# Chunk inverses of a gated linear attention stored as 32x32 blocks, and applied by 32-row, 32-column matmuls

## The chip, the cores and the metric

The kernel runs on one core of a Trainium2 chip. The core has a matrix engine (TensorE, PE in the profile, with its weight loads as PEld), a vector engine (VectorE, DVE), a scalar engine (ScalarE, ACT), GpSimd (POOL), and DMA queues, some of them issued by SyncE (SP). The engines run on their own and meet at semaphores. The metric is the time of one execution in microseconds (us) on the device; lower is better.

## The reference

A recurrent attention over 768 tokens for 4 x 8 heads of 40 dimensions, followed by a mixture of 8 experts over the 3,072 tokens that it gives. Cut to what matters:

```python
for t in range(S):                      # S = 768
    y[:, :, t] = einsum('bhd,bhde->bhe', rt, state)
    Sa = einsum('bhde,bhe->bhd', state, at)
    state_decay = state * wt[:, :, None, :] - einsum('bhd,bhe->bhde', Sa, bt)
    state = state_decay + einsum('bhd,bhe->bhde', vt, kt)
...
x = attn_out.transpose(0, 2, 1, 3).reshape(B * S, H * D)
# tokens with x @ w_skip > 0 go to their best expert:
h = np.maximum(xc[mask] @ w1[e], 0.0)
out[do_compute] = xc + gate_w[mask, None] * (h @ w2[e])
```

## The kernel before, in words

The 768 tokens are worked in 24 chunks of 32. Within a chunk the recurrence becomes matrix products, but for one thing: token t removes what the earlier tokens of its chunk have already removed. That is a triangular system of 32x32 per head and chunk, and its inverse is computed once and then applied to a block of right-hand sides. A chunk has 32 such systems (4 batches x 8 heads). The heads go as two halves, x = 0 and x = 1, of four heads each, and in each half four 32x32 inverses of one head, one for each batch, are applied together.

**The inverse.** `tinv` (L210) is a generator that makes the inverses of two pairs of chunks (one phase, four chunks) by elimination on VectorE: thirty steps of a product (L228) and a subtraction (L230), spread over the chunks by calls of `T()`, each of which takes one step. Batches lie on the partitions in blocks of 32. At the end ScalarE copies a piece (L232), and L237 transposes the result into the tiles `TBa`. `TBa[q]` holds the inverses of one pair of chunks, [128 partitions, 16, 128]: entry [p, h, m] is a 128x128 matrix for each h, with the four 32x32 inverses of the batches on its diagonal and zeros elsewhere. L237 takes one batch at a time: it reads 32 partitions and writes them into their 32 columns of both tiles. What is left of the generator when a phase ends is run at once (`run_all(tg)`), so the transposes stand between the end of one phase's last chunk and the start of the next phase. The zeros off the diagonal were put there at the start: by ScalarE for `TBa[0]` (L391), by GpSimd for `TBa[1]` (L425) and for `TBa[2]` (L540, in chunk 2). The inverses of the first phase come from `tinv0` (L239), whose parts `full` (L271) and `s2` (L275) copy pieces into `TBa` with VectorE and ScalarE in turn.

**Applying it.** For chunk c and half x, in this order: `rs` (L284) multiplies the state with r, its result copied by VectorE (L296) or ScalarE (L297); `ux` (L299) makes the right-hand sides (L306), copied by ScalarE (L308); `uq` (L310) applies the inverse (L315): four matmuls, one per head, with the whole 128x128 block-diagonal matrix as weights and 72 columns moving; ScalarE copies the result out in four pieces (L317) and GpSimd masks a part of it (L319); `sst` (L320) makes the new state (L327, L332), copied by L336, L337 and L340; `yy` (L342) makes the output (L350, L354). A matmul in fp32 shows as two matmul and two weight-load instructions in the profile.

**The order.** TensorE, ScalarE and VectorE run what is written, in the order in which it is written, chunk by chunk in the loop from L469 on; no scheduler moves anything. Between the steps of the chain lie the preparation of later chunks (L163 and its transposes L174, `kbt` L185 and L188, `wtt` L197, `m2` L207, scans L114 and L126, GpSimd's L143, L151 and L170) and the routing of finished tokens to the experts (`route`, called by `RP`: L632, L640, L675, L676 on TensorE, L648 to L685 on VectorE, the scattered write L688 on GpSimd). `warm` and `zb` (L358) are matmuls with no use of their own. The experts (L786, L797) follow after the last chunk.

Names in the profile: `TB` the inverses, `M` a work area, `UXs` the copied right-hand sides, `pc`, `ps`, `py`, `pq`, `px` PSUM banks, `R1t` and `L2t` operands of the chain, `SS` the state.

## Time and profile before

| what | value |
|---|---|
| timed runs, median (lowest to highest of 3) | 689.55 us (689.51 to 695.32) |
| profiled execution: its time, its span | 686.84 us, 685.0 us |
| granted TensorE clock, mean | 0.842 |
| busy: PE, PEld | 553.0 us (81%), 473.5 us (69%) |
| busy: DVE, ACT, POOL | 516.1 us (75%), 422.7 us (62%), 324.2 us (47%) |
| instructions | 31,223, of them 13,620 matmuls |
| attention, about | 0 to 540 us of the span |
| experts, about | 540 to 685 us |

The profile was taken of one execution, and the durations in the text are of that execution. Its time is the span and 1.8 us around it. In the tables by line a row reads: line, engine, operation, written tile <- read tiles, shapes, count, then busy time in us, mean ns of one instruction, idle time of the engine ahead of them and what ended it. In the stretches in order of time the two numbers ahead are the start and the length in us, and what stands in brackets is the engine's idle time ahead of the row and what ended it. The chain of work that ended last is followed back from the end of the program: at each step to what released it, or to the instruction ahead of it on its engine. The granted clock is 1 at the full speed of TensorE and 0.5 at the half; it changes between these two during the attention.

### The profile page before, as it was taken

Reading aid. Unit: us, or ns where it says so; the run is one execution under the profiler, and the core shown is the slowest. Engines: PE = TensorE matmul, PEld = TensorE weight load, DVE = VectorE, ACT = ScalarE, POOL = GpSimd, SP = SyncE. Lnnn points to the kernel's source line nnn. Section 1 sums busy time; section 2 is a strip of 40 time slices with the busy share of each in tenths; the row PEclk is TensorE's granted clock in tenths of the full one; section 3 lists DMA queues with packets and bytes.
Section 4 is the critical chain, followed back from the end, with each engine's and each line's share of the span. In section 5 each row is a group of like instructions: output and inputs, shape, how many; then the busy total and the mean of one; then the engine's idle time right before and its main releaser. Section 6 shows DMA issues by size and latency. Waiting matters only on the chain.

```text
span 685.0 us, 31223 instructions
## 1 busy us (share of the span) xinstructions
PE 553.0 (81%) x13620; PEld 473.5 (69%) x13620; DVE 516.1 (75%) x1201; ACT 422.7 (62%) x1154; POOL 324.2 (47%) x248
## 2 busy tenths in 40 slices
PE   5678586778776789866898678997978799999995
PEld 2445475667665668655787567776767689999995
DVE  7999678876997779977699774785339366889881
ACT  6545564576864758747687475877686454444540
POOL 5483942736546365463554533131322236666661
PEclk9788878578996777969779687798897999999998
DMA  7672755352443514435244242435256347677210
GB/s 185 185 239 98 194 138 180 109 161 58 125 132 102 163 50 121 141 102 166 60 129 131 73 126 71 104 110 185 73 158 170 108 127 221 215 214 226 87 49 23
DMA packets 67437, 90.91 MB, mean 133 GB/s; under 512 B 32564, under 2 KB 54657, under 8 KB 65806
## 3 DMA queue, kind: packets, MB, share of 16 engines
q1 hardware_dynamic: 62350, 74.05, 37.2%
q0 software_dynamic: 4944, 14.80, 6.8%
q8 instruction: 109, 1.79, 1.1%
q14 instruction: 34, 0.28, 0.1%
HBM read 74.03 MB, written 17.08 MB: 133 GB/s over the span
## 4 chain that ended last, share of the span: by engine, by line
PE 37%; DVE 29%; ACT 11%; issue 10%; DMA 4%; POOL 3%; POOLq 0%; DVEq 0%; ACTq 0%
DVE M L228 5%; PE pc L786 4%; PE pc L315 4%; PE ps L797 4%; DVE M L126 4%; DVE TB L237 4%; ACT R1t L317 3%; PE ps L327 3%; PE pc L306 3%; PE px L786 2%; PE pc L292 2%; DVE M L230 2%; PE py L797 2%; PE ps L332 2%; ACT L2t L188 2%
## 5 line engine op out<-in xcount | busy, mean ns | idle before, releaser
L319 POOL TENSOR_TENSOR R1t<-R1t,mc 64x512 f32<-64x512 f32 x46 | 62.2, 1353 | 152.2 <-ACT R1t L317 123.7
L317 ACT COPY R1t<-pc 32x288 f32<-32x288 f32 x192 | 74.8, 389 | 30.6 <-PE pc L315 27.5
L315 PE MATMUL pc<-UXs,TB 128*128 128x72 f32 x384 | 66.4, 328 | 0.1
L143 POOL TENSOR_TENSOR WR<-WR,M 128x1024 f32<-128x1024 f32 (+1 forms) x19 | 52.0, 2748 | 23.0 <-DVE M L114 16.9
L734 POOL TENSOR_TENSOR WL<-WR,WH 128x1280 fp32r<-128x1280 f32 (+1 forms) x21 | 57.6, 2779 | 8.7 <-ACT WH L733 8.6
L327 PE MATMUL ps<-R1t,L2t 128*40 128x40 f32 x1472 | 52.4, 228 | 10.9 <-ACT R1t L317 5.1
L315 PEld LDWEIGHTS pc<-UXs,TB 128*128 128x128 f32 x384 | 58.8, 234 | 3.4 <-issue 1.0
L188 ACT COPY L2t<-pq 64x160 f32<-64x160 f32 x184 | 52.6, 286 | 7.0 <-PE pq L185 4.7
L327 PEld LDWEIGHTS ps<-R1t,L2t 128*40 128x40 f32 x1472 | 42.7, 139 | 20.3 <-ACT R1t L317 11.7
L209 ACT COPY R1t<-pq 32x128 f32<-32x128 f32 x184 | 47.0, 256 | 6.5 <-issue 3.0
L228 DVE TENSOR_TENSOR M<-M 128x22 f32<-128x22 f32 (+10 forms) x110 | 49.7, 452 | 0.0
L237 DVE STREAM_TRANSPOSE TB<-M 32x1024 f32<-32x1024 f32 x20 | 38.4, 1919 | 13.7 <-ACT M L232 13.5
L292 PE MATMUL pc<-rvt,SS 128*40 128x32 f32 x1472 | 44.9, 218 | 3.7 <-issue 3.6
L340 ACT COPY SS<-ps 40x320 f32<-40x320 f32 x92 | 38.6, 419 | 14.5 <-PE ps L332 13.0
L688 POOL DMA_INDIRECT xg<-XS,ix x24 | 25.0, 1040 | 46.5 <-DMA xg<-XS,ix 20.9
L292 PEld LDWEIGHTS pc<-rvt,SS 128*40 128x40 f32 x1472 | 38.6, 137 | 11.7 <-issue 8.7
L332 PE MATMUL ps<-L2t,R1t 128*40 128x40 f32 x1472 | 42.7, 220 | 0.4 <-issue 0.4
L308 ACT COPY UXs<-pc 128x288 f32<-128x288 f32 x48 | 19.2, 400 | 36.1 <-PE pc L306 32.1
L230 DVE TENSOR_TENSOR px<-px,M 128x168 f32<-128x168 f32 (+8 forms) x150 | 39.1, 261 | 1.4
L733 ACT CAST WH<-WR 128x1024 fp32r<-128x1024 f32 (+1 forms) x35 | 39.6, 1132 | 0.0
L332 PEld LDWEIGHTS ps<-L2t,R1t 128*40 128x40 f32 x1472 | 38.8, 136 | 0.5 <-issue 0.5
L228 DVE TENSOR_TENSOR M<-M,px 128x168 f32<-128x168 f32 (+8 forms) x150 | 37.0, 247 | 1.7
(244 smaller groups left out, 1577.5 us busy)
## 6 DMA issues: line engine op xcount, KB each, us to landing
rvt<-rv POOLq DMA_DIRECT2D x21, 512.0 KB, 4.6
WR<-kb SPq DMA_DIRECT2D x10, 1024.0 KB
WR<-w SPq DMA_DIRECT2D x16, 640.0 KB
WR<-w SPq DMA_DIRECT2D x16, 512.0 KB
M<-wt SPq DMA_DIRECT2D x9, 520.5 KB
M<-at SPq DMA_DIRECT2D x8, 512.0 KB
WR<-w SPq DMA_DIRECT2D x16, 256.0 KB
R1t<-vt SPq DMA_DIRECT2D x48, 80.0 KB
```

The source lines that it names most:

```text
L143: E.tensor_tensor(H[h]['KB'][0:NR(h),:,:,q,:],H[h]['KB'][0:NR(h),:,:,q,:],v4(Wi)[0:NR(h)],ALU.mult)
L188: A.copy(L2[x][h%NL2][64-64*x:128-64*x,c,bb*4:bb*4+4,:],pt[64*c:64*c+64,:,64*x:64*x+40])
L228: V.tensor_tensor(tv,NLt[:,j,j+1:32].unsqueeze(2).broadcast_to([128,n,k]),X[:,j,lo:hi].unsqueeze(1).broadcast_to([128,n,k]),ALU.mult)
L230: for tv,xv in q: V.tensor_tensor(xv,xv,tv,ALU.subtract)
L237: V.transpose(d.rearrange("p h (x f) m -> p m x h f",x=2)[:,q],Xi[q])
L292: TE.matmul(RS[s,v,:],SS[x][:,b//2,v,:],rr[:,b%2,2*hh+x,:],start=True,stop=True)
L315: TE.matmul(UQ[:,hh,:],Tb[:,x*8+hh*2+c%2,:],UXd[x][:,hh,:],start=True,stop=True)
L317: A.copy(R[uu,4*b:4*b+4,:],UQ[32*b:32*b+32,:,:])
L319: (V if c==NC-1 else G).tensor_tensor(R[pq,:,40:72],R[pq,:,40:72],mQ[pq].unsqueeze(1).broadcast_to([64,16,32]),ALU.mult)
L327: TE.matmul(ST[s,v,:],l2[:,cc,u,:],R[:,u,0:40],start=True,stop=True)
L332: TE.matmul(S2[s,v,:],R[:,u,0:40],l2[:,cc,u,:],start=True,stop=True)
L734: def low(s,E,o,x,h): E.tensor_tensor(s.R(o),x,h,ALU.subtract)
```

## The change

The inverses are kept as 32x32 blocks without the zeros around them: `TBa[q]` is [128, 16, 32], a quarter of the size, and entry [p, h, m] holds batch p // 32's inverse alone. `uq` issues sixteen matmuls for four: for each head and each batch b one with the 32 rows and 32 columns at 32b, on the diagonal of the array. L237's four transposes of 32 partitions become one of 128, with one step of the generator for four, and with writes that lie 32 elements apart instead of 128. `full` copies all 128 partitions with one VectorE copy for four copies (two of them on ScalarE in its first call). With no zeros to keep, the three clearings of `TBa` go. Scratch that had lain in `TBa[2]` before it was first used lies in a tile of its own, `SCR`.

```diff
-    TB=cp.tile([128,NTB*2048],F32,name="TB")
-    TBa=[TB[:,2048*q:2048*q+2048].rearrange("p (h m) -> p h m",h=16) for q in range(NTB)]
+    TB=cp.tile([128,NTB*512],F32,name="TB"); SCR=cp.tile([128,2048],F32,name="SCR")
+    TBa=[TB[:,512*q:512*q+512].rearrange("p (h m) -> p h m",h=16) for q in range(NTB)]
...
         s0=(2*ph)%NTB; s1=(2*ph+1)%NTB
-        for b in range(4):
-            q=slice(32*b,32*b+32)
-            t0=TBa[s0]; d=bass.AP(t0.tensor,t0[q].offset,(tuple(t0[q].ap[0]),(TBa[s1].offset-t0.offset,2),(128,16),(1,128)))
-            V.transpose(d.rearrange("p h (x f) m -> p m x h f",x=2)[:,q],Xi[q])
-            yield
+        t0=TBa[s0]; d=bass.AP(t0.tensor,t0.offset,(tuple(t0.ap[0]),(TBa[s1].offset-t0.offset,2),(32,16),(1,32)))
+        V.transpose(d.rearrange("p h (x f) m -> p m x h f",x=2),Xi)
+        yield
...
-        DB=TBa[2][:,12:16].rearrange("p h m -> p (h m)").rearrange("p (a b) -> p a b",a=16)
+        DB=SCR[:,1536:2048].rearrange("p (a b) -> p a b",a=16)
...
-        def full(w,E):
-            for b in range(4):
-                q=slice(32*b,32*b+32)
-                (V.tensor_copy,A.copy)[E[b]](TBa[w][q,:,q].rearrange("p (x f) m -> p x f m",x=2),NLt[q].rearrange("p m (x h f) -> p h x f m",x=2,h=2)[:,w])
+        def full(w):
+            V.tensor_copy(TBa[w].rearrange("p (x f) m -> p x f m",x=2),NLt.rearrange("p m (x h f) -> p h x f m",x=2,h=2)[:,w])
...
         for hh in range(4):
-            TE.matmul(UQ[:,hh,:],Tb[:,x*8+hh*2+c%2,:],UXd[x][:,hh,:],start=True,stop=True)
+            for b in range(4):
+                q=slice(32*b,32*b+32)
+                TE.matmul(UQ[q,hh,:],Tb[q,x*8+hh*2+c%2,:],UXd[x][q,hh,:],start=True,stop=True)
...
-            zero(fT(0))
...
-            G.memset(fT(1),0.0); G.memset(z[:,512:640],0.0); G.memset(L1t[:,2048:3072],0.0)
+            G.memset(z[:,512:640],0.0); G.memset(L1t[:,2048:3072],0.0)
...
-            full(0,(0,1,0,1))
+            full(0)
...
-            if c==1: full(1,(0,0,0,0)); m1(3,0,0); m1(3,0,1)
+            if c==1: full(1); m1(3,0,0); m1(3,0,1)
...
-            if c==2: s2(1,1,(0,0,1,1)); G.memset(TBa[2],0.0)
+            if c==2: s2(1,1,(0,0,1,1))
```

On VectorE, where chunk 7 ends and chunk 8 begins (230 us in the profile), the order before was as follows; the transposes write `TB`, the rows on `R1t` are evacuations of the chain, and those on `pos`, `base`, `sl` and `ix` are the routing:

```order
L354 TENSOR_TENSOR XS<-py_103,WT 128x320
L237 STREAM_TRANSPOSE TB<-M 32x32x2x2x8
L336 TENSOR_TENSOR R1t<-ps_102,D_977 40x8x40 x2
L237 STREAM_TRANSPOSE TB<-M 32x32x2x2x8 x3
L680 TENSOR_TENSOR pos<-pq_105,base 128x8
L681 TENSOR_TENSOR base<-pq_105,base 128x8
L680 TENSOR_TENSOR pos<-pq_105,base 128x8
```

And at the same place in the changed kernel, whose lines have other numbers (L235 is the transpose, L334 what was L336, L676 and L677 what were L680 and L681):

```order
L352 TENSOR_TENSOR XS<-py_103,WT 128x320
L235 STREAM_TRANSPOSE TB<-M 128x32x2x2x8
L334 TENSOR_TENSOR R1t<-ps_102,D_985 40x8x40 x2
L676 TENSOR_TENSOR pos<-pq_105,base 128x8
L677 TENSOR_TENSOR base<-pq_105,base 128x8
L676 TENSOR_TENSOR pos<-pq_105,base 128x8
```

The one transpose stands where the first of the four stood, and the three behind the evacuation are gone; all else keeps its order.

On TensorE, at the start of chunk 8, the order before, in which L315 applies the inverse for the second half of chunk 7 (each row is one matmul of the program, times the count):

```order
L676 MATMUL pq_105<-oh,mc 32x16 x4
L292 MATMUL pc_100<-rvt,SS_115 40x32 x16
L163 MATMUL pq_104<-WR,L1t 32x64 x16
L315 MATMUL pc_99<-UXs,TB 128x72 x4
L197 MATMUL pq_105<-mc,WE 128x104 x4
L350 MATMUL py_103<-L2t,R1t 32x40 x16
L632 MATMUL pq_104<-mc,XS 128x128 x2
```

And in the changed kernel (L313 is what was L315):

```order
L672 MATMUL pq_105<-oh,mc 32x16 x4
L288 MATMUL pc_100<-rvt,SS_116 40x32 x16
L163 MATMUL pq_104<-WR,L1t 32x64 x16
L313 MATMUL pc_99<-UXs,TB 32x72 x16
L197 MATMUL pq_105<-mc,WE 128x104 x4
L348 MATMUL py_103<-L2t,R1t 32x40 x16
L628 MATMUL pq_104<-mc,XS 128x128 x2
```

Sixteen matmuls of 32x72 stand where four of 128x72 stood, between the same neighbours.

## The prediction

> **What bounds the kernel now.** I read the chain of work that ended last first, then one of its stretches in order of time, and then the same stretch on all engines. The chain, by engine and by line:

> ```profile
> PE 37%; DVE 29%; ACT 11%; issue 10%; DMA 4%; POOL 3%; POOLq 0%; DVEq 0%; ACTq 0%
> by line: issue 9.9%; DVE M L228 5.0%; PE pc L786 4.2%; PE pc L315 4.2%; PE ps L797 4.1%; DVE M L126 3.9%; DVE TB L237 3.7%; ACT R1t L317 3.4%; PE ps L327 3.3%; PE pc L306 2.8%; PE px L786 2.5%; PE pc L292 2.4%; DVE M L230 2.2%; PE py L797 2
> ```

> No engine is the bound by itself; the chain hops between TensorE, VectorE and ScalarE. Both lines that the change rewrites stand on it: L315, the matmuls that apply the inverse, with 4.2% of 685.0 us = 28.8 us, and L237, the transposes that write the inverse out, with 3.7% = 25.3 us. The groups of the same trace (count | busy us, mean ns), with a third line to measure L237 by:

> ```profile
> L315 PE MATMUL pc<-UXs,TB 128*128 128x72 f32 x384 | 66.4, 328 | 0.1
> L237 DVE STREAM_TRANSPOSE TB<-M 32x1024 f32<-32x1024 f32 x20 | 38.4, 1919 | 13.7 <-ACT M L232 13.5
> L213 DVE STREAM_TRANSPOSE M<-M 128x1024 f32<-128x1024 f32 x5 | 6.1, 1211 | 0.0
> ```

> So 25.3 of L237's 38.4 us are on the chain. The twenty transposes come as four at each of five places, where one pair of chunks ends and the next begins (144, 230, 316, 400 and 472 us). The second of them, all engines, start and duration in us:

> ```profile
> 229.98 0.37 ACT L232 COPY M<-px 128x256 f32<-128x256 f32 x1
> 230.38 1.91 DVE L237 STREAM_TRANSPOSE TB<-M 32x1024 f32<-32x1024 f32 x1 [3.03 <-ACT M L232]
> 232.16 0.95 DVE L336 TENSOR_TENSOR R1t<-ps,D 40x320 f32<-40x320 f32 x2
> 233.13 5.79 DVE L237 STREAM_TRANSPOSE TB<-M 32x1024 f32<-32x1024 f32 x3
> 233.22 0.29 PE L676 MATMUL pq<-oh,mc 128*32 128x16 f32 x8
> 233.44 1.28 PE L292 MATMUL pc<-rvt,SS 128*40 128x32 f32 x32
> 234.65 1.08 PE L163 MATMUL pq<-WR,L1t 128*32 128x64 f32 x32
> 235.66 1.99 PE L315 MATMUL pc<-UXs,TB 128*128 128x72 f32 x8
> 238.94 0.17 DVE L680 TENSOR_TENSOR pos<-pq,base 128x8 f32<-128x8 f32 x1
> 239.50 0.96 PE L197 MATMUL pq<-mc,WE 104*128 104x104 f32 x4 [1.85 <-DVE base L681]
> 240.39 0.76 PE L350 MATMUL py<-L2t,R1t 128*32 128x40 f32 x32
> 240.98 0.85 DVE L296 TENSOR_TENSOR R1t<-pc,D 40x256 f32<-40x256 f32 x2
> 242.23 0.90 PE L632 MATMUL pq<-mc,XS 128*128 128x128 f32 x3 [1.08 <-DVE M L174]
> 243.07 1.19 PE L306 MATMUL pc<-R1t,WR 128*32 128x72 f32 x32
> ```

> VectorE is busy with transposes until 238.92; the routing step L680 and L681, whose input (L676) was there at 233.51, queues behind them. TensorE has run ahead, finishes L315 at 237.65, and waits 1.85 us for L681; L296, which feeds the next chunk's first matmuls L306, is late for the same reason. The place is VectorE's.

> **The change, part by part.** *The transposes.* Four instructions of 32 partitions become one of 128 with as many elements each. The trace has no transpose of 128 partitions into this layout: L237 itself (1.92 us, scattered writes) and L213 (1.21 us, contiguous) are the nearest on either side. I take 1.92 us, since the writes stay scattered, only 32 elements apart instead of 128. VectorE is then rid of 3 x 1.92 = 5.8 us at each place: 28.8 us of busy time.

> Not all of that is worth time, since TensorE is close behind. In the stretch above the one transpose ends at 230.38 + 1.92 = 232.30, L336 at 233.3, the routing steps L680 to L685 took 240.98 - 238.94 = 2.04 us and end at 233.51 + 2.04 = 235.6, L296 at 236.4. The end is now set on TensorE, which goes on from L315 at 235.66: the new L315 (1.19 us at this clock, below), L197 0.96, L350 0.76, L632 0.90, so L306 starts at 239.47 instead of 243.07: 3.6 us. For the other places, L315 and L306:

> ```profile
> 149.22 1.98 PE L315 MATMUL pc<-UXs,TB 128*128 128x72 f32 x8
> 156.62 1.19 PE L306 MATMUL pc<-R1t,L1t 128*32 128x72 f32 x32
> 321.09 1.11 PE L315 MATMUL pc<-UXs,TB 128*128 128x72 f32 x8
> 327.86 1.19 PE L306 MATMUL pc<-R1t,L1t 128*32 128x72 f32 x32
> 405.75 1.57 PE L315 MATMUL pc<-UXs,TB 128*128 128x72 f32 x8
> 412.73 1.19 PE L306 MATMUL pc<-R1t,WR 128*32 128x72 f32 x32
> 475.72 0.78 PE L197 MATMUL pq<-mc,WE 104*128 104x104 f32 x3 [2.93 <-issue]
> ```

> The same 3.81 us behind L315 give 3.6, 3.0 and 3.2 us. The fifth place is held by TensorE's own wait at 475.72, so there I count only the shorter L315, 0.8 us. Together 3.6 + 3.6 + 3.0 + 3.2 + 0.8 = 14.2 us. At the full clock the 3.81 us would shrink, at most to some 2.4, which bounds the term at 20; if ScalarE's queue holds TensorE back by a further us at each place, it is 10.

> *The matmuls.* An old step is 4 matmuls of 128x128 weights, 8 instructions; a new one is 16 of 32x32, 32 instructions. Nothing in the trace has exactly that shape, but L306 has the same count and the same 72 moving columns, with four column tiles in turn. Both, at the full and at the half clock:

> ```profile
> 223.88 1.11 PE L315 MATMUL pc<-UXs,TB 128*128 128x72 f32 x8
> 229.80 0.71 PE L306 MATMUL pc<-R1t,L1t 128*32 128x72 f32 x32
> ```

> Full: 1.11 becomes 0.71, 0.40 saved. Half (rows at 235.66 and 243.07 above): 1.99 becomes 1.19, 0.80 saved. That is 36% and 40% of a step, and so 0.38 x 28.8 = 10.9 us if all of L315's share of the chain follows; 0.8 of it is counted already. TensorE's order is fixed and the steps beside it often wait for somebody else (L306 for VectorE, L327 for ScalarE's L317), so I take two thirds of 10.1, 6.7 us, with 3.4 and 10.1 as the ends.

> Is L306 a fair price? It uses four column strips and all rows; the new matmuls use four different row strips and four column strips, and all four write into one PSUM bank. The chunk-inverse start-up has just that diagonal pattern, with 16 columns (L269); the warm-up matmuls give the time per column without tiles:

> ```profile
> 60.35 1.29 PE L269 MATMUL pq<-M 32*16 32x16 f32 x128
> 66.67 2.84 PE L358 MATMUL ps<-mc 128*128 128x512 f32 x6
> ```

> L358 takes 2.84 / 6 = 0.47 us for 512 columns, 0.92 ns a column. Sixteen columns one after another would be 14.8 ns; L269 starts one every (1.29 - 0.18) / 127 = 8.7 ns. So diagonal tiles overlap. [...]

> *Instructions.* TensorE gets 48 x 24 = 1,152 more matmul instructions on 13,620, and as many weight loads. It stops at times with nothing to wait for, as 2.93 us in the row at 475.72. One such stop more is 2.9 us, none is 0; I take 1.5 us lost.

> *Start-up.* L274's copies become one for each half. The second half stands on VectorE while GpSimd's small L132 copies are on the chain:

> ```profile
> 76.57 2.36 DVE L274 COPY TB<-M 32x512 f32<-32x512 f32 x4
> ```

> ```profile
> 77.22 0.56 POOL D L132
> 79.02 0.18 POOL D L132
> ```

> L132 takes 0.56 us beside L274 and 0.18 without it. Three of the four copies go, with one L132 beside each: 3 x (0.56 - 0.18) = 1.1 us gained, between 0 and 1.5. The cleared TB areas go too. I price them at nothing: ScalarE's 1.89 us lie before a 5.91 us idle stretch, GpSimd's at L425 before one of 12.75 us, and the one at L540 stands between its own steps at 127 us, with nobody waiting; without that cover they would be worth 1.8 us each.

> ```profile
> 19.73 0.60 ACT L165 COPY M<-pq 128x128 f32<-128x128 f32 x2 [5.91 <-issue]
> 62.21 2.90 POOL L319 TENSOR_TENSOR R1t<-R1t,mc 64x512 f32<-64x512 f32 x1 [12.75 <-issue]
> 126.82 1.83 POOL L540 MEMSET TB<- 128x2048 f32 x1
> ```

> The sum: 14.2 + 6.7 + 1.1 - 1.5 = 20.5 us off the profiled execution's 686.84, that is 666.3. That execution lies 2.7 us below the median of the timed runs, 689.55; against the median, 669.0. With all ends the gain is 10 + 3.4 + 0 - 2.9 = 10.5 to 20 + 10.1 + 1.5 = 31.6 us: 658 to 679.

> **The rivals.** *Row tiles do not overlap (slower).* If the four diagonal matmuls ran one after another, a column at 0.92 ns, a step would take 32 x 72 x 0.92 ns = 2.1 us at the full clock and twice that at the half: 1.4 and 3.0 us over my 0.71 and 1.19. The 28.8 us on the chain are about 19 steps of 1.5 us, and four more lie at the places above, so each 0.1 us a step costs 2.3 us. At a mean of 2.2 us over, 51 us are lost against 20.5 gained: 720. It decides from about 0.9 us over, where the gain is used up: an instruction every 45 ns at the full clock instead of 16. For it: no row shows 32x32 tiles with 72 columns. Against it: L269. Chance 0.05.

> *The clock.* In two stages (length, TensorE busy, ..., then the granted clock):

> ```profile
> 230.00:316.00 86.00, 68.62 (x2064) 58.53 (x2059) 71.03 (x187) 57.85 (x176) 43.31 (x36) 0.76 0.39 116
> 540.00:685.00 145.00, 133.37 (x1099) 127.45 (x1087) 100.55 (x146) 63.27 (x92) 75.30 (x39) 0.98 0.47 143
> ```

> The clock stood at 0.98 where TensorE was busy for 92% of the stage and at 0.76 where it was for 80%. Some 130 of the chain's 253 us on TensorE (37% of 685) lie before the last stage. If smaller matmuls cost clock, 0.76 to 0.68, these take 130 x (0.76 / 0.68 - 1) = 15 us more: a gain of 5, 684; chance 0.06. The reverse: TensorE no longer idles 1.85 us and more at the five places, and the half clock behind them (L306 1.19 instead of 0.71) stays away for some six groups of 0.48 us each: 14 us more gained, 655; chance 0.12. Busy time speaks for neither: per stage about 5 us go from 68.6 and about 5 from 86, which leaves 0.79 against 0.80.

> *Another chain is close behind.* ScalarE's L317 copies and GpSimd's L319 follow each step unchanged. If they eat half of the first term and all of the second, 7 + 1 - 1.5 = 6.5 us are left: 683. Chance 0.15.

> **How the numbers follow.** Forecast 0.62 (658 to 679), more clock 0.12 (655), close chain 0.15 (683), less clock 0.06 (684), no overlap 0.05 (720). The range 654 to 682 holds the first two and leaves out most of the rest. One per cent, about what a measurement of this kernel can tell from no change, is 6.9 us: faster means below 682.7. The first two cases and about half of the close chain are faster, 0.81; its other half and nearly all of less clock are the same, 0.13; slower is 0.06.

> **What would show it.** Right: five transposes of 128x1024 near 1.9 us each; L680 starting as soon as L676 and L336 are done; TensorE going from the inverse matmuls to L197 without a wait for VectorE; those steps at 0.7 and 1.2 us. Wrong: steps of 2 us and more, a granted clock under 0.70 in 230 to 316, or a ScalarE wait of several us in the place of VectorE's.

## The result and the profile after

The changed kernel takes 663.96 us (median of 4 runs, 661.24 to 667.34) against 691.1 us for the kernel before, run beside it (689.51 to 695.32): a ratio of 0.960, 95% interval 0.954 to 0.967. Run again in a later comparison it took 665.85 us against 689.88, a ratio of 0.966 (0.959 to 0.973). The gain is 24 to 27 us, 3.4 to 4%. Ratios leave disturbed runs out, which matters for one kernel below, the one with twelve short extra matmuls: two of its four runs are left out, and its ratio answers to 677 us where the median of all four is 682.43. The profiled execution took 663.83 us, with a span of 662.1 us: 23.0 us below the profiled execution of before.

More lines of the changed kernel have new numbers: L302 was L306, L292 was L296, L330 was L332, L348 was L350. The first rows of its page, with the row of the queue that brings instructions (packets, MB, share):

```profile
span 662.1 us, 33508 instructions
PE 515.5 (78%) x14772; PEld 432.2 (65%) x14772; DVE 489.7 (74%) x1182; ACT 419.5 (63%) x1151; POOL 324.2 (49%) x246
q8 instruction: 118, 1.93, 1.2%
```

The chain of work that ended last can be followed back in this trace only to 315 us, so its shares cannot be set beside those of before. TensorE's busy time fell by 37.5 us although it has 1,152 more matmul instructions, and VectorE's by 26.4 us. The instruction queue brought 9 packets more than the row below, from the page of before:

```profile
q8 instruction: 109, 1.79, 1.1%
```

1.93 MB in 118 packets is 16.4 KB each, and 1,152 matmuls over 9 packets are 128 a packet: with the weight load of each, 256 of TensorE's instructions for each packet. Two kernels below agree: with 1,152 matmul instructions more than the changed kernel the queue brings 127 packets, with 588 fewer 113. The number comes back below.

The rewritten groups of the changed kernel:

```profile
L313 PE MATMUL pc<-UXs,TB 32*32 32x72 f32 x1536 | 43.1, 255 | 6.0 <-issue 5.9
L235 DVE STREAM_TRANSPOSE TB<-M 128x1024 f32<-128x1024 f32 x5 | 9.8, 1960 | 13.9 <-ACT M L232 13.9
```

The inverse matmuls went from 66.4 to 43.1 us; the transposes from 38.4 to 9.8, and one of 128 partitions, at 1.96 us, costs what one of 32 did (1.92). Now the second phase end, where chunk 7 gives way to chunk 8, in order of time. It answers to the stretch at 230 us of before:

```profile
220.78 0.37 ACT L232 COPY M<-px 128x256 f32<-128x256 f32 x1
221.18 1.96 DVE L235 STREAM_TRANSPOSE TB<-M 128x1024 f32<-128x1024 f32 x1 [3.04 <-ACT M L232]
222.98 0.96 DVE L334 TENSOR_TENSOR R1t<-ps,D 40x320 f32<-40x320 f32 x2
...
223.98 0.23 PE L672 MATMUL pq<-oh,mc 128*32 128x16 f32 x8
...
224.35 0.17 DVE L676 TENSOR_TENSOR pos<-pq,base 128x8 f32<-128x8 f32 x1 [0.42 <-PE pq L672]
...
225.47 0.86 DVE L292 TENSOR_TENSOR R1t<-pc,D 40x256 f32<-40x256 f32 x2
...
226.43 1.18 PE L313 MATMUL pc<-UXs,TB 32*32 32x72 f32 x32
227.54 0.58 PE L197 MATMUL pq<-mc,WE 104*128 104x104 f32 x4
228.05 0.34 PE L348 MATMUL py<-L2t,R1t 128*32 128x40 f32 x14
230.40 0.40 PE L348 MATMUL py<-L2t,R1t 128*32 128x40 f32 x18 [2.00 <-issue]
230.73 0.71 PE L628 MATMUL pq<-mc,XS 128*128 128x128 f32 x3
231.37 1.19 PE L302 MATMUL pc<-R1t,WR 128*32 128x72 f32 x32
```

The routing step L676 now starts as soon as L672 has its sums, with VectorE idle ahead of it; L313 runs straight into L197, where TensorE had waited 1.85 us for L681. From the first transpose to L302 it is 231.37 - 221.18 = 10.19 us, where before it was 243.07 - 230.38 = 12.69. So 2.5 us came of the 3.6 forecast for this place; a new stop of 2.00 us, in the middle of L348 and ended by nothing the profile shows, fell into the gap.

The same two things over the whole run, in the list of TensorE's waits (who waits <- for what: us in total, times, longest). Before:

```profile
PE pc L306 <- DVE R1t L296: 17.7, 7, 4.4
PE pq L197 <- DVE base L681: 9.4, 4, 3.2
PE pq L163 <- issue: 3.9, 6, 1.4
PE py L350 <- issue: 3.7, 2, 2.6
```

After:

```profile
PE pc L302 <- DVE R1t L292: 11.0, 7, 2.9
PE pq L163 <- issue: 11.1, 10, 3.3
PE py L348 <- issue: 8.6, 7, 2.0
PE ps L330 <- issue: 6.4, 4, 3.5
```

The wait for the routing's `base` is gone from the list, and the one of L306 for L296 is 6.7 us shorter: 16.1 us together. (In the second profile of the changed kernel the latter is 14.2 us, 3.5 shorter.) Of all of TensorE's waits for VectorE, 64 us became 46 in both profiles. Stops that nothing explains grew from 25.0 to 53.4 us in total (47.1 in the second profile of the same kernel). That is where the change costs time, and the experiments below are mostly about it.

### The profile page after: what moved, and what is told of

It reads as the page before. It is cut to its first block, busy times and chain, and to the rows that moved or that the text cites. A ratio compares the mean times of both kernels' runs of the same rounds, so it can differ in the third digit from the quotient of the medians.

```text
span 662.1 us, 33508 instructions
## 1 busy us (share of the span) xinstructions
PE 515.5 (78%) x14772; PEld 432.2 (65%) x14772; DVE 489.7 (74%) x1182; ACT 419.5 (63%) x1151; POOL 324.2 (49%) x246
## 3 DMA queue, kind: packets, MB, share of 16 engines
q8 instruction: 118, 1.93, 1.2%
## 4 chain that ended last, share of the span: by engine, by line
PE 24%; DVE 11%; ACT 8%; issue 5%; DMA 2%; POOL 1%; SPq 0%; POOLq 0%; DVEq 0%; ACTq 0%
PE pc L782 5%; PE ps L793 4%; PE px L782 3%; ACT R1t L315 2%; PE py L793 2%; ACT L2t L188 2%; DVE M L228 2%; PE ps L325 2%; DVE ti L789 2%; PE pc L313 1%; PE pc L288 1%; DVE M L230 1%; PE ps L330 1%; ACT SS L338 1%; ACT R1t L209 1%
## 5 line engine op out<-in xcount | busy, mean ns | idle before, releaser
L317 POOL TENSOR_TENSOR R1t<-R1t,mc 64x512 f32<-64x512 f32 x46 | 60.5, 1315 | 104.7 <-ACT R1t L315 72.6
L315 ACT COPY R1t<-pc 32x288 f32<-32x288 f32 x192 | 74.9, 390 | 20.7 <-PE pc L313 17.6
L325 PE MATMUL ps<-R1t,L2t 128*40 128x40 f32 x1472 | 48.2, 221 | 11.0 <-issue 5.3
L143 POOL TENSOR_TENSOR WR<-WR,M 128x1024 f32<-128x1024 f32 (+1 forms) x19 | 44.2, 2332 | 25.8 <-DVE M L114 19.7
L228 DVE TENSOR_TENSOR M<-M 128x22 f32<-128x22 f32 (+10 forms) x110 | 55.0, 500 | 0.0
L325 PEld LDWEIGHTS ps<-R1t,L2t 128*40 128x40 f32 x1472 | 39.3, 132 | 18.9 <-ACT R1t L315 8.9
L330 PE MATMUL ps<-L2t,R1t 128*40 128x40 f32 x1472 | 42.9, 218 | 6.5 <-issue 6.4
L313 PE MATMUL pc<-UXs,TB 32*32 32x72 f32 x1536 | 43.1, 255 | 6.0 <-issue 5.9
L330 PEld LDWEIGHTS ps<-L2t,R1t 128*40 128x40 f32 x1472 | 38.2, 134 | 7.3 <-issue 7.2
L230 DVE TENSOR_TENSOR M<-M 128x22 f32<-128x22 f32 (+10 forms) x110 | 40.8, 371 | 0.0
L230 DVE TENSOR_TENSOR px<-px,M 128x168 f32<-128x168 f32 (+8 forms) x150 | 39.1, 260 | 1.4
L313 PEld LDWEIGHTS pc<-UXs,TB 32*32 32x32 f32 x1536 | 32.1, 122 | 11.4 <-issue 8.9
L789 DVE CAST ti<-xe 128x2 int32<-128x2 f32 x8 | 39.3, 4911 | 0.2
L174 DVE STREAM_TRANSPOSE M<-pq 128x128 f32<-128x128 f32 x40 | 12.1, 308 | 36.9 <-ACT M L165 24.3
```

The source lines that it names most:

```text
L228: V.tensor_tensor(tv,NLt[:,j,j+1:32].unsqueeze(2).broadcast_to([128,n,k]),X[:,j,lo:hi].unsqueeze(1).broadcast_to([128,n,k]),ALU.mult)
L230: for tv,xv in q: V.tensor_tensor(xv,xv,tv,ALU.subtract)
L313: TE.matmul(UQ[q,hh,:],Tb[q,x*8+hh*2+c%2,:],UXd[x][q,hh,:],start=True,stop=True)
L315: A.copy(R[uu,4*b:4*b+4,:],UQ[32*b:32*b+32,:,:])
L317: (V if c==NC-1 else G).tensor_tensor(R[pq,:,40:72],R[pq,:,40:72],mQ[pq].unsqueeze(1).broadcast_to([64,16,32]),ALU.mult)
L325: TE.matmul(ST[s,v,:],l2[:,cc,u,:],R[:,u,0:40],start=True,stop=True)
```

## Experiments

The line numbers of before hold for the first two kernels, those of the changed kernel (shifted by a few where lines were added) for the others. Each time is a median beside runs of the kernel before on the same chip: 688.42 us in the comparison with the first four, 689.88 with the next four, 690.33 with the last three.

### One part alone: the matmuls

The kernel before, with `uq` as sixteen 32x32 matmuls that read the blocks out of the wide, zero-filled tiles. Four transposes, clearings and copies stay.

```diff
         for hh in range(4):
-            TE.matmul(UQ[:,hh,:],Tb[:,x*8+hh*2+c%2,:],UXd[x][:,hh,:],start=True,stop=True)
+            for b in range(4):
+                q=slice(32*b,32*b+32)
+                TE.matmul(UQ[q,hh,:],Tb[q,x*8+hh*2+c%2,q],UXd[x][q,hh,:],start=True,stop=True)
```

> The kernel before with the sixteen 32x32 matmuls alone (weights cut out of the wide block-diagonal tiles; four transposes, start-up and clearings as before). My theory: shorter matmuls are worth little by themselves, because TensorE gets 1,152 more matmul instructions and waits for instruction blocks more often (its idle time with no releaser goes from 25 us to 45 us or more), and because VectorE still holds the phase ends: 686 to 692 us against 690. The prediction's own terms (6.7 less 1.5) would give 685. The rival, that the matmuls carry the gain: 680 or less.

681.83 us, a ratio of 0.989 (0.982 to 0.997): 6.6 us gained, with some 2 to 12 as the interval. The matmuls alone help, by about the forecast's net of 6.7 - 1.5 = 5.2, and the expectation of 686 to 692 failed; the unexplained stops came to 40.2 us, where it said 45 or more. That they are waits for blocks of instructions is its theory; what the traces show of it stands at the end. At the second phase end the four transposes and the wait behind them are as before:

```profile
225.63 5.78 DVE L237 STREAM_TRANSPOSE TB<-M 32x1024 f32<-32x1024 f32 x3
231.99 0.95 PE L197 MATMUL pq<-mc,WE 104*128 104x104 f32 x4 [2.68 <-DVE base L683]
```

### One part alone: the transposes

The kernel before with three of the four transposes of each place left out, so the inverses of batches 1 to 3 are not written behind the first phase. The 128x128 matmuls stay.

```diff
-        for b in range(4):
+        for b in range(1):
             q=slice(32*b,32*b+32)
```

> The kernel before with one of the four transposes at each phase end left out of four (one of 32 partitions runs, three are left out, so three batches keep stale inverses). Nothing else is changed. My theory: the phase ends carry most of the gain, 672 to 677 us (14 to 18 us off, as in the prediction's first term or a little over). The rival, that the matmuls carry it: 683 or more.

673.69 us, 0.978 (0.970 to 0.986): 14.7 us, beside the 14.2 of the forecast's first term. The two are not quite the same thing. The 14.2 us count on the shorter inverse matmul at each place, which this kernel does not have; with L315 as long as before, the prediction's rows give 2.8, 2.8, 3.0, 2.8 and 0 us for the five places, 11.4 together. From the first transpose of a place to the next L306, its profile takes 3.6, 3.1, 3.5, 2.8 and 3.1 us less than that of before, 16.1 together. So the fifth place, priced at nothing but the shorter L315, gives as much as the others. It begins and ends here, and in the profile of before at 472.31 and 482.77:

```profile
461.84 1.91 DVE L237 STREAM_TRANSPOSE TB<-M 32x1024 f32<-32x1024 f32 x1 [2.53 <-ACT M L232]
469.21 0.84 PE L306 MATMUL pc<-R1t,L1t 128*32 128x72 f32 x32
```

At the second place TensorE stops in the middle of L350, as it does in L348 of the changed kernel:

```profile
234.07 0.61 PE L350 MATMUL py<-L2t,R1t 128*32 128x40 f32 x19 [1.68 <-issue]
```

### The same from the other side: four transposes in the changed kernel

```diff
-        t0=TBa[s0]; d=bass.AP(t0.tensor,t0.offset,(tuple(t0.ap[0]),(TBa[s1].offset-t0.offset,2),(32,16),(1,32)))
-        V.transpose(d.rearrange("p h (x f) m -> p m x h f",x=2),Xi)
-        yield
+        for b in range(4):
+            q=slice(32*b,32*b+32)
+            t0=TBa[s0]; d=bass.AP(t0.tensor,t0[q].offset,(tuple(t0[q].ap[0]),(TBa[s1].offset-t0.offset,2),(32,16),(1,32)))
+            V.transpose(d.rearrange("p h (x f) m -> p m x h f",x=2),Xi[q])
+            yield
```

> The changed kernel with its one transpose split again into four of 32 partitions, into the narrow tiles. My theory: VectorE holds the phase ends again, some 14 to 18 us of the 27 are lost: 677 to 682 us. The rival (matmuls carry the gain): below 670.

681.51 us, 0.989 (0.982 to 0.997): 16 to 17.5 us more than the changed kernel's 665.85 and 663.96, and the wait is back where it was.

```profile
226.85 5.79 DVE L237 STREAM_TRANSPOSE TB<-M 32x1024 f32<-32x1024 f32 x3
233.22 0.96 PE L197 MATMUL pq<-mc,WE 104*128 104x104 f32 x4 [3.61 <-DVE base L679]
```

This kernel has the small matmuls and the narrow tiles and stands where the matmuls alone stood (681.83). So the larger part of the gain is the transposes', from either side.

### The start-up

The changed kernel with the old start-up: four copies for each half, two of them on ScalarE, and the three clearings, of a tile that nothing reads.

```diff
-    TB=cp.tile([128,NTB*512],F32,name="TB"); SCR=cp.tile([128,2048],F32,name="SCR")
+    TB=cp.tile([128,NTB*512],F32,name="TB"); SCR=cp.tile([128,2048],F32,name="SCR"); DUM=cp.tile([128,2048],F32,name="DUM")
...
-        def full(w):
-            V.tensor_copy(TBa[w].rearrange("p (x f) m -> p x f m",x=2),NLt.rearrange("p m (x h f) -> p h x f m",x=2,h=2)[:,w])
+        def full(w,E):
+            for b in range(4):
+                q=slice(32*b,32*b+32)
+                (V.tensor_copy,A.copy)[E[b]](TBa[w][q].rearrange("p (x f) m -> p x f m",x=2),NLt[q].rearrange("p m (x h f) -> p h x f m",x=2,h=2)[:,w])
...
+            zero(DUM)
...
-            G.memset(z[:,512:640],0.0); G.memset(L1t[:,2048:3072],0.0)
+            G.memset(DUM,0.0); G.memset(z[:,512:640],0.0); G.memset(L1t[:,2048:3072],0.0)
...
-            full(0)
+            full(0,(0,1,0,1))
...
-            if c==1: full(1); m1(3,0,0); m1(3,0,1)
+            if c==1: full(1,(0,0,0,0)); m1(3,0,0); m1(3,0,1)
...
-            if c==2: s2(1,1,(0,0,1,1))
+            if c==2: s2(1,1,(0,0,1,1)); G.memset(DUM,0.0)
```

> The changed kernel with the start-up work of before: four copies in each half of the start-up inverse, and three clearings of the old size (of a tile that nothing reads). The prediction's term: 1.1 us lost, 665. The rival, read from the trace (chunk 1's first inverse step begins 5.3 us earlier after the change): 4 to 7 us lost, 668 to 671.

664.22 us, 0.964 (0.956 to 0.971): no difference from 663.96 and 665.85. A loss of 4 to 7 us is ruled out; one of 1.1 us would be too small to tell from nothing in these runs.

### What the extra instructions cost

Two kernels with nearly the same extra array work in each of the 48 steps of `uq` and very different counts: twelve extra matmuls of one column, or one extra matmul of 112 columns. What they add goes to a part of the PSUM tile that nothing reads. Both are edits of the changed kernel, whose own time in this comparison is 665.85 us.

> The changed kernel once more, as the base of the three beside it: 661 to 667 us.

```diff
-        UQ=ps_c.tile([128,4,72],F32,tag="pc",name="psUQ")
+        UQf=ps_c.tile([128,512],F32,tag="pc",name="psUQ"); UQ=UQf[:,0:288].rearrange("p (a b) -> p a b",a=4)
...
+        for k in range(12):
+            q=slice(32*(k%4),32*(k%4)+32)
+            TE.matmul(UQf[q,288+k:289+k],Tb[q,x*8+c%2,:],UXd[x][q,0,k:k+1],start=True,stop=True)
```

> The changed kernel with twelve more 32x32 matmuls of one moving column at each inverse step, into unused PSUM columns: 24 matmul instructions and 24 weight loads, some 24 x 8.7 ns = 0.2 us of array time. If TensorE is held by the supply of instructions: 8 to 15 us slower than the changed kernel, and the idle time of TensorE with no releaser rises from 53 us to 75 or more. If only array time counts: 2 to 5 us slower, as the next kernel.

A ratio of 0.981 (0.974 to 0.989), that is 677 us (682.43 as the median of all four, from 674.6 to 687.2): 11 us more than the changed kernel. The unexplained stops came to 71.6 us in its profile, a run of 687.18 us; 75 or more were expected. And with one long matmul in their place:

```diff
+        TE.matmul(UQf[0:32,288:400],Tb[0:32,x*8+c%2,:],UXd[x][0:32].rearrange("p h n -> p (h n)")[:,0:112],start=True,stop=True)
```

> The changed kernel with one more 32x32 matmul of 112 moving columns at each inverse step: 2 matmul instructions and 2 weight loads, some 2 x 103 ns = 0.2 us of array time, as in the kernel beside it. Supply of instructions: 1 to 4 us slower than the changed kernel, clearly less than the short ones. Array time alone: the same as the short ones.

670.29 us, 0.973 (0.968 to 0.977), that is 671 us by the ratio: 4.4 us more, a little over the 1 to 4 expected. The added groups, the short ones first and the long one in the second fence (of the first row only the count and the busy time are used):

```profile
L316 PE MATMUL pc<-UXs,TB 32*32 32x1 f32 x1152 | 19.5, 170 | 14.1 <-issue 14.1
```

```profile
L314 PE MATMUL pc<-UXs,TB 32*32 32x112 f32 x96 | 20.7, 299 | 2.0 <-issue 2.0
```

Busy for 19.5 and 20.7 us, they differ by 1,056 instructions and, by the ratios, by 6 us: some 6 ns an instruction that the matmuls' busy time does not account for. The two intervals overlap, so the size is loose. The weight loads differ too (busy for 18.1 and 10.0 us beside the matmuls), and this pair does not take them apart from the supply of instructions. For the change's 1,152, small matmuls at the same places, it makes some 7 us.

### Fewer instructions elsewhere

The routing's scores and ranks, in both kernels four matmuls of 32 columns of weights each, as one of 128: 588 matmul instructions fewer.

```diff
-            for q in range(4): nc.tensor.matmul(lg[32*q:32*q+32],xT[:b-a,k,32*q:32*q+32],s.wg[:b-a,k,:],start=k==0,stop=k==2)
+            nc.tensor.matmul(lg,xT[:b-a,k],s.wg[:b-a,k,:],start=k==0,stop=k==2)
...
-        for q in range(4): nc.tensor.matmul(rk[32*q:32*q+32,0:n,:],s.tri[:,32*q:32*q+32],oh,start=True,stop=True)
-        for q in range(4): nc.tensor.matmul(rk[32*q:32*q+32,n:2*n,:],s.one[:,0:32],oh,start=True,stop=True)
+        nc.tensor.matmul(rk[:,0:n,:],s.tri,oh,start=True,stop=True)
+        nc.tensor.matmul(rk[:,n:2*n,:],s.one,oh,start=True,stop=True)
```

> The changed kernel with the routing's small matmuls made wide: scores by 3 matmuls of 128-column weights for 12 of 32, ranks by 2 for 8; 588 matmul instructions less, and some 0.5 to 1 us more array time for each routing. Supply of instructions: 2 to 8 us faster than the changed kernel. Array time alone: 0 to 8 us slower.

676.26 us, 0.979 (0.973 to 0.986): 10.4 us slower than the changed kernel, outside both expectations. The unexplained stops did shrink, from 47.1 to 35.6 us, but the wide matmuls took more than that. The scores in this kernel, and then in the changed kernel's second profile:

```profile
L636 PE MATMUL pq<-wg,xT 128*128 128x9 f32 x96 | 17.5, 292 | 4.8 <-ACT WT L199 4.8
L636 PE MATMUL pq<-wg,xT 64*128 64x9 f32 x48 | 10.7, 294 | 0.0
```

```profile
L636 PE MATMUL pq<-wg,xT 128*32 128x9 f32 x384 | 8.1, 189 | 4.4 <-ACT WT L199 4.4
L636 PE MATMUL pq<-wg,xT 64*32 64x9 f32 x192 | 6.2, 191 | 0.0
```

A quarter of the instructions, twice the busy time: 28.2 for 14.3 us. A weight load of 128x128 took 227 ns in the mean, for 118 ns at 128x32 in the changed kernel's first profile, and a matmul 292 ns for 189; that the loads make the difference is the author's guess, and was not tried apart. The granted clock was lower as well, 0.845 to 0.863 for 0.869 to 0.888. So this run tells of wide weights and not of the count; the next two keep the tiles small and lower the count.

### The same matmuls in fewer instructions

The changed kernel with one matmul for two heads (8 of 144 columns a step) and for four (4 of 288 columns). Array work and tiles stay; the second head of a pair, and in the other kernel three of four heads, get a neighbour's inverse, so the computation is not the reference's.

```diff
-        for hh in range(4):
+        for hh in range(0,4,2):
             for b in range(4):
                 q=slice(32*b,32*b+32)
-                TE.matmul(UQ[q,hh,:],Tb[q,x*8+hh*2+c%2,:],UXd[x][q,hh,:],start=True,stop=True)
+                TE.matmul(UQ[q,hh:hh+2,:],Tb[q,x*8+hh*2+c%2,:],UXd[x][q,hh:hh+2,:],start=True,stop=True)
```

> The changed kernel with two heads in each inverse matmul: 8 matmuls of 144 moving columns for 16 of 72, so 768 matmul instructions less and the same columns through the array. Half of the heads get their neighbour's inverse (left out: half of the applied inverses). Supply of instructions: from the short and long extras (1,056 more instructions cost some 12 us at the same array time) some 9 us faster than the changed kernel, 655 to 659 us. If only columns count: 663 to 666.

659.05 us, 0.953 (0.948 to 0.959).

```diff
-        for hh in range(4):
+        for hh in range(0,4,4):
             for b in range(4):
                 q=slice(32*b,32*b+32)
-                TE.matmul(UQ[q,hh,:],Tb[q,x*8+hh*2+c%2,:],UXd[x][q,hh,:],start=True,stop=True)
+                TE.matmul(UQ[q,hh:hh+4,:],Tb[q,x*8+hh*2+c%2,:],UXd[x][q,hh:hh+4,:],start=True,stop=True)
```

> The changed kernel with all four heads in each inverse matmul: 4 matmuls of 288 moving columns, 1,152 matmul instructions less, as many as the kernel before has (left out: three of four heads' inverses, the first one's is applied to all). Supply of instructions: some 13 us faster than the changed kernel, 650 to 655 us, with the idle time of TensorE with no releaser back near 25 to 30 us. If only columns count: 663 to 666.

655.39 us, 0.949 (0.943 to 0.956). Eight matmuls a step, then four (one fence each):

```profile
L313 PE MATMUL pc<-UXs,TB 32*32 32x144 f32 x768 | 41.2, 334 | 1.4 <-issue 1.3
```

```profile
L313 PE MATMUL pc<-UXs,TB 32*32 32x288 f32 x384 | 40.7, 493 | 0.9 <-issue 0.8
```

The busy time hardly moves (43.1, 41.2, 40.7 us), and a step of the last kernel is 40.7 / 48 = 0.85 us in the mean, for 0.90 in the changed kernel, while the time falls by 5 to 7 and by 9 to 10 us and the unexplained stops fall from 47 to 53 us to 35.5 and 28.7. The last kernel has exactly the 13,620 matmuls of before. So the 1,152 extra instructions cost 8.6 to 10.5 us (663.96 and 665.85 less 655.39) by this kernel, 7 to 11 by the ratios, beside the 7 of the pair above. The runs of the three kernels do not overlap: 652.9 to 658.1, 658.3 to 659.9, and 661.2 or more for the changed kernel.

### Is VectorE still late at the phase ends?

The changed kernel with no transposes there at all: the inverses of every phase but the first are left out.

```diff
-        V.transpose(d.rearrange("p h (x f) m -> p m x h f",x=2),Xi)
         yield
...
-            if c==2: s2(1,1,(0,0,1,1))
+            if c==2: s2(1,1,(0,0,1,1)); G.memset(TBa[2],0.0)
```

> The changed kernel without the five transposes at the phase ends (left out: the inverses of all phases but the first; one clearing of a tile is put in). If TensorE and its instructions hold the phase ends since the change, as the trace has it, at most 3 us faster than the changed kernel: 661 to 665 us. If VectorE still holds them: 655 or less.

665.24 us, 0.963 (0.957 to 0.968): nothing more. The five transposes that remain cost nothing that these runs can tell: 9.8 us off VectorE's queue do not show.

## Why the prediction was right, and where it was not

The forecast was 669.0 us with a range of 654 to 682; measured were 664 and 666. Term by term:

- **Phase ends, 14.2 us.** Right in cause, and by the medians some 2 to 3 us short in size. Three transposes of four are worth 14.7 us alone, where the forecast without shorter inverse matmuls is 11.4, and 16 to 17.5 us from the other side, where it is 14.2. What was short is above all the fifth place: that it is "held by TensorE's own wait at 475.72" did not hold, it gave 3.1 us. What the prediction said would show it is there: five transposes of 1.96 us, L676 starting when L672 is done, no wait of L197 for `base`. Its own limit, "TensorE is close behind", held too: without any transpose nothing more comes. At the second place 2.5 of the 3.6 us came, with a stop in L348 in the gap.
- **The steps, 0.71 and 1.19 us.** Right: L313 took 0.70 us at the full clock and 1.18 us at the half, as in the stretch above and in the row below.

```profile
235.84 0.70 PE L313 MATMUL pc<-UXs,TB 32*32 32x72 f32 x32
```

- **No overlap of row tiles (the slower rival).** It fell. The four diagonal tiles write one PSUM tile, `pc`, and 32 of their matmuls took 0.70 us, where one after another, at the 0.92 ns a column of L358, would have been 2.1. From start to start that is (0.70 - 0.22) / 31 = 15.5 ns, with the 0.22 us that the trace has as L313's median. The 16 ns in the prediction's rival are L306's by the same sum from its row of before, (0.71 - 0.23) / 31.
- **The matmuls, 6.7 us gained and 1.5 us lost to instructions.** The net came out, 5.2 forecast and 6.6 measured, but by luck: both terms were too small, and the errors cancel. One step that failed is "one such stop more is 2.9 us, none is 0; I take 1.5 us lost": the extra instructions cost 8.6 to 10.5 us, or 7 to 11 by the ratios. The gain ahead of that is 6.6 + 7 to 6.6 + 11, some 14 to 18 us. Two kernels above bear it out: both have 13,620 matmul instructions and one transpose at each place, one with the wide matmuls (673.69 us) and one with the small (655.39), and they lie 18 us apart, 20 by the ratios. Either way it is above the stated 3.4 to 10.1. L315's share of the chain was taken as the most that could be won, and was not. Chains close behind it can have become shorter too, and the clock rose, as the next point says; how the 4 to 10 us above the upper end split between these two is open. The term also takes off only 0.8 us for what the phase ends had counted already, where the prediction's own rows have 2.8 (14.2 less 11.4).
- **The clock.** The rival in which it falls fell itself. It rose, as in the other, but not for the reason given there. In the timed runs the mean granted clock was 0.823 to 0.855 for the kernel before and 0.869 to 0.894 for the changed one. With the matmuls alone it was 0.860 to 0.879, with the transposes alone 0.836 to 0.850: it comes with the small matmuls and not with the idle time at the phase ends. From 230 to 316 us of the profile it was 0.86 after 0.76, with TensorE busy for 75% of the stretch after 80%, so TensorE's busy share does not explain it. Why it rose is not settled.
- **Start-up, 1.1 us.** Nothing that shows. The L197 of chunk 1 came 1.9 us earlier in the trace (77.41 for 79.33 us), but the old start-up put into the changed kernel makes no difference in the time. Where the 1.9 us go was not followed, and 1.1 us is too little for these runs.
- **Another chain close behind.** The rival named ScalarE and GpSimd. What came close was TensorE itself, with its work at the phase ends (665.24 us without any transpose there) and with its instructions (655.39 us with 1,152 fewer).
- **The parts together.** Singly they gain 6.6 + 14.7 = 21.3 us, together 24 to 27. The forecast's sum took them as independent; 3 to 6 us more were not foreseen, about as much as the intervals leave uncertain, and no run takes them apart.

## What to carry to other kernels

When wide matmuls are cut into array tiles, count the instructions as well as the columns: here each extra small matmul instruction cost some 6 to 10 ns over its array time, which took about half of what the tiles had won. Saving instructions by wide weights was no way out here, with 9 columns moving (10.4 us slower). More columns for each small weight were, in kernels that leave out part of the inverses: 4.9 to 6.8 us faster with 144 columns, 8.6 to 10.5 with 288. Shortening VectorE's queue at the phase ends paid (14.7 us for three transposes of four) until TensorE was the late one, and then nothing more (665.24 us without the last transpose too). Which engine comes next can be read beforehand from the same stretch of the trace, and leaving the rest of that work out altogether tells whether the place is used up.

## What the runs showed of the hardware

In six stretches of the changed kernel's profile, given below, TensorE's stops without a cause in the profile lie 127 to 129 matmuls apart. The first stop in the stretch at 88 us falls between the 5th and the 6th of the 32 instructions of an L313 step, the next one inside L348:

```profile
85.80 0.31 PE L313 MATMUL pc<-UXs,TB 32*32 32x72 f32 x5
88.37 0.69 PE L313 MATMUL pc<-UXs,TB 32*32 32x72 f32 x27 [2.26 <-issue]
...
91.82 0.49 PE L348 MATMUL py<-L2t,R1t 128*32 128x40 f32 x31 [0.72 <-issue]
```

Six stretches from the end of one stop to the end of the next (start:end, length, then busy time and count of PE, PEld, DVE, ACT and POOL, granted clock, DMA share, GB/s):

```profile
88.37:91.82 3.45, 2.73 (x128) 2.34 (x128) 3.14 (x15) 2.62 (x8) 1.63 (x2) 1.00 0.46 89
91.82:96.02 4.20, 2.98 (x128) 2.57 (x128) 4.16 (x18) 3.22 (x11) 0.40 (x1) 1.00 0.55 176
149.99:153.54 3.55, 2.40 (x129) 2.12 (x129) 2.37 (x5) 1.99 (x6) 2.67 (x3) 1.00 0.08 25
153.54:157.63 4.09, 2.56 (x128) 2.16 (x127) 4.05 (x2) 3.56 (x11) 4.09 (x2) 1.00 0.05 12
270.10:273.83 3.73, 2.56 (x128) 2.34 (x128) 3.65 (x17) 2.22 (x6) 1.31 (x2) 1.00 0.11 39
273.83:277.81 3.98, 2.35 (x127) 1.99 (x127) 3.82 (x8) 3.17 (x11) 1.32 (x2) 1.00 0.19 52
```

Counted by packets, most have no stop of over 0.4 us: 17 stops on 109 packets before the change, 40 on 118 after it. Where small matmuls come in bursts the stops cost time all the same: those with no other cause in the profile grew from 25.0 us to 47 to 53 us, and fewer instructions for the same array work brought 8.6 to 10.5 us.
